# Softcap attention with a two-way maxout layer: w2's last two parts loaded in f32 and cast on VectorE, w1's loads spread, the w2 w_out product in another order

## Chip, cores and metric

One core of one Trainium2 chip. The metric is the time of one execution on the device, in microseconds (us): the median over runs of the same kernel. The engines are named as the profile names them: PE (TensorE, matrix products), PEld (its weight loads), DVE (VectorE), ACT (ScalarE), POOL (GpSimd), SP (SyncE, which here only issues transfers).

## The reference

For each of 8 batches and 12 heads (448 rows, head size 64): `scores = 30 * tanh(q k^T / 8 / 30)`, a softmax over the keys, times `v`. The heads are put side by side into `x` of 3584 x 768. Then, with `w1` and `w2` of 768 x 1024 and `w_out` of 1024 x 768:

```python
h1 = x @ w1
h2 = x @ w2
g = np.maximum(h1, h2)
return (g @ w_out).astype(np.float32)
```

Inputs and output are float32.

## The kernel before

**The second layer is rewritten.** max(h1, h2) = h2 + relu(h1 - h2), so the output is x (w2 w_out) + relu(x (w1 - w2)) w_out. The kernel makes the two weight matrices once, at the start: `wd_sb` = w1 - w2 in bf16 (`subtract`, L224, on POOL, one instruction for each of KC = 6 parts of 128 rows) and `wm_sb` = w2 w_out (`premultiply`, L237, on PE: 16 matmuls for a part, in two halves of 8, each evicted by DVE at L248). A part of w2 must be turned before it can be the weight operand: `turn_w2` (L229) is 8 transposes on PE into one PSUM tile "mm" and a DVE copy into `w2T` (L235). "mm" and `w2T` have two buffers each, so a new half can only start when the eviction two tiles back is done.

**Where the weights lie.** w2 in bf16 (`w2b`) borrows the one buffer of `gT`, which the second layer's relu (L410) writes later. w1 in f32 has no tiles of its own: parts 0 to 3 (OB = 4) lie in the four "osb" buffers, parts 4 and 5 in the first "xT" buffer (`w1x`). w2 comes by POOL's software queue, which casts on the way (L216); w_out too (L207); w1 by SP (L222).

**Attention.** The 48 pairs of heads are taken in 24 steps t of two pairs, and q, k, v are loaded, cast to bf16 and turned in groups g of three pairs (0 and 1 in wide rows, the others as rows of 768 and 256 bytes, L130 to L143). Groups 0 and 1 are turned on PE (L273). From group 2 on, POOL casts k and q (L183 to L195) and SP starts a DMA transpose, the crossbar (`cross`, L279), which fills `qkT`; the step's score matmuls (L306, L301) wait for it. Step 3 is the first that needs group 2, and the second tile of step 4 the first that needs group 3. ACT takes tanh (L307, L309) and exp (L314) of each tile; `total` (L343) and `values` (L364) make the row sums and the products with v on PE, DVE normalizes (L394) into `xT`.

**What sets the order.** The schedule is written out by hand: every engine runs its instructions in program order, and waits only by data and buffers. Filler work for PE sits in a list `fill_q` of generators, and `F(n)` takes n matmuls from its head. In the first steps the list holds turn and premultiply of parts 1 to 5, turn always one part ahead; from step 2 on the second layer is appended (L406 is x times `wd_sb`, whose first tile reads all six parts one after another; L418 and L421 make the output; L425 evicts it).

**SP's queue around the change:** k, q, v of groups 0 and 1; k and q of group 2; all six parts of w1 (L519); the transpose of group 2 (L565); k, q of group 3; v of group 2; the transpose of group 3 (L595); v of group 3; the groups 4 and 5. Each of SP's transfers also waits for the one eight places before it, since they share eight semaphores in turn.

**POOL's queue around the change:** issue of w2 parts 0 and 1 and of w_out (L490 to L493); casts of group 1; issue of w2 parts 2 to 5 (L513); v of groups 0 and 1; k, q of group 2; subtract parts 0 to 3 (L624); k, q of group 3; subtract parts 4 and 5 (L596); v of groups 2 and 3; then, after a one-element copy that waits for a step's `xT` (`mark`, L641), the next groups.

Of the kernel before, what the change touches and what calls it, by code (L numbers as in the profile page):

```python
# [10 lines left out]
def kernel(  # L11
# [11 lines left out]
    nc = tc.nc  # L23
    f32 = mybir.dt.float32
# [7 lines left out]
    DF = moe_w1.shape[1]  # L32
    P = 128
# [85 lines left out]
    def load(g, what, n0=0, n1=L):  # L119
        b, p = divmod(g * L, NP)  # L120
        h0, h1 = 2 * (p + n0), 2 * (p + n1)
        src = {"k": k, "q": q, "v": v}[what]
        t, m, l = raw_of(g, what)
        if g < NT:
            nc.sync.dma_start(
                out=t[:, n0 * S : n1 * S].rearrange("p (n c) -> p n c", c=S),
                in_=rows(src, b, h0, h1).rearrange("(n p) c -> p n c", p=P),
            )
            return
        nc.sync.dma_start(  # L130
            out=m[:, 2 * n0 : 2 * n1, :],
            in_=src[b, h0:h1, 0 : NJ * P, :].rearrange("h (p j) d -> p h (j d)", j=NJ),
        )
        if what == "q":
            nc.sync.dma_start(
                out=l[half(b), 2 * n0 : 2 * n1, :],
                in_=src[b, h0:h1, NJ * P : S, :].rearrange("h p d -> p h d"),
            )
        else:
            for par in range(2):  # L140
                nc.sync.dma_start(
                    out=l[64 * par : 64 * par + 64, n0:n1, :],
                    in_=src[b, h0 + par : h1 : 2, NJ * P : S, :].rearrange("h p d -> p h d"),  # L143
                )
# [72 lines left out]

    w1x = xpool.tile([P, NP, 2 * S], bf16, name="xT").rearrange("p c s -> p (c s)").bitcast(f32)

    def load_w1(c):  # L220
        w1_in[c] = opool.tile([P, DF], f32, name="osb") if c < OB else w1x[:, (c - OB) * DF : (c - OB + 1) * DF]
        nc.sync.dma_start(out=w1_in[c], in_=x_rows(moe_w1, c))  # L222

    def subtract(c, eng=nc.vector):  # L224
# [4 lines left out]
    def turn_w2(c):  # L229
        ps = mm_psum.tile([P, 512], f32, name="mm").bitcast(bf16)  # L230
        for f in range(FC):
            nc.tensor.transpose(ps[:, f * P : (f + 1) * P], w2b[:, c, f * P : (f + 1) * P], ident)
            yield
        w2T[c] = stage.tile([P, FC * P], bf16, name="w2T", bufs=2)
        nc.vector.tensor_copy(w2T[c], ps)  # L235

    def premultiply(c):  # L237

        for half in range(2):
            hs = slice(half * (DM // 2), (half + 1) * (DM // 2))  # L240
            ps = mm_psum.tile([P, 512], f32, name="mm")
            for f in range(FC):
                nc.tensor.matmul(  # L243
                    ps[:, : DM // 2], w2T[c][:, f * P : (f + 1) * P], wo_sb[:, f, hs],
                    start=(f == 0), stop=(f == FC - 1),
                )
                yield
            nc.vector.tensor_copy(wm_sb[:, c, hs], ps[:, : DM // 2])  # L248
# [149 lines left out]
    def moe(b):  # L398
        if b % 2 == 0:
            gT[b // 2] = xpool.tile([P, FC, 2 * S], bf16, name="gT", bufs=1)  # L400
        g, x = gT[b // 2], xT[b // 2]
        cs = slice((b % 2) * S, (b % 2 + 1) * S)
        for f in range(FC):
            ps = mm_psum.tile([P, 512], f32, name="mm")
            for c in range(KC):
                nc.tensor.matmul(  # L406
                    ps[:, :S], wd_sb[:, c, f * P : (f + 1) * P], x[:, c, cs], start=(c == 0), stop=(c == KC - 1)
                )
                yield
            nc.vector.tensor_relu(g[:, f, cs], ps[:, :S])  # L410
        for t in range(3) if b % 2 == 0 else range(3, 7):
            osb = opool.tile([P, DF], f32, name="osb")[:, :DM]
            ts = slice(t * P, (t + 1) * P)
            for half in range(2):
                hs = slice(half * (DM // 2), (half + 1) * (DM // 2))
                ps = mm_psum.tile([P, 512], f32, name="mm")
                for c in range(KC):
                    nc.tensor.matmul(ps[:, : DM // 2], x[:, c, ts], wm_sb[:, c, hs], start=(c == 0), stop=False)  # L418
                    yield
                for f in range(FC):  # L420
                    nc.tensor.matmul(  # L421
                        ps[:, : DM // 2], g[:, f, ts], wo_sb[:, f, hs], start=False, stop=(f == FC - 1)
                    )
                    yield
                nc.vector.tensor_copy(osb[:, hs], ps[:, : DM // 2])  # L425
                if b == B - 1 and t == 6:
                    o = out[b * S : b * S + NJ * P, hs].rearrange("(p j) n -> p j n", j=NJ)
                    nc.sync.dma_start(out=o[:, NJ - 1, :], in_=osb[:, hs])
            if b == B - 1 and t == 6:
                continue  # L430
            wide = b * NP >= NT * L
            if t == 3:
                for n in range(2):
                    o = out[(b - 1 + n) * S : (b + n) * S, :]
                    to = o[NJ * P : S, :] if (b - 1 + n) * NP >= NT * L else o.rearrange("(r j) n -> r j n", j=R7)[:, R7 - 1, :]
                    nc.sync.dma_start(out=to, in_=osb[64 * n : 64 * n + 64, :])
            else:
                j = t if t < 3 else t - 4
                o = out[b * S : (b + 1) * S, :]
                if wide:  # L440
                    nc.sync.dma_start(out=o[: NJ * P, :].rearrange("(p j) n -> p j n", j=NJ)[:, j, :], in_=osb)
                else:
                    o = o.rearrange("(r j) n -> r j n", j=R7)
                    for n in range(2):
                        nc.sync.dma_start(out=o[:, 2 * j + n, :], in_=osb[64 * n : 64 * n + 64, :])
# [4 lines left out]
    def F(n):  # L450
        rate[1] += n * rate[0]
        while rate[1] >= 1 and fill_q:
            try:
                next(fill_q[0])
                rate[1] -= 1
            except StopIteration:
                fill_q.pop(0)
        if not fill_q:
            rate[1] = 0.0
# [50 lines left out]
    ex(0, 3)  # L510
    cast(nc.gpsimd, 1, "k")
    cast(nc.gpsimd, 1, "q")
    for c in range(2, KC):  # L513
        load_w2(c)
    cast(nc.gpsimd, 0, "v", halves=(1,))
    load(1, "v")
    load(2, "k")
    load(2, "q")
    for c in range(KC):  # L519
        load_w1(c)  # L520

    first = {}

# [41 lines left out]
    cross(2)  # L565
    load(3, "k")
    load(3, "q")
    load(2, "v")
    premultiply_first(6, 8)
    for c in range(1, KC):  # L570
        if c + 1 < KC:
            fill_q.append(turn_w2(c + 1))
        fill_q.append(premultiply(c))
    scores(2, 0)
    ex(1, 3)
    total(0)
# [4 lines left out]
    for t in range(1, NQ):  # L581
        i = 2 * t
        more = t + 1 < NQ
        F(24 if t == 2 else 0)
        if t > 1 and more:
            scores(t + 1, 0)
        if t > 1:
            ex(t, 3)
            F(6)
        if t in crosses:  # L590
            cross(crosses[t])
        if t == 2:
            cast(nc.gpsimd, 3, "k")
            cast(nc.gpsimd, 3, "q")
            cross(3)  # L595
            for c in range(4, KC):  # L596
                subtract(c, nc.gpsimd)
        if t == 3:
            cast(nc.gpsimd, 3, "v")
        if t > 2:  # L600
            extra(i)
        F(8 if t > 1 else 0)
        add(t, 1, 0)
        F(2 if t > 1 else 0)
        if more:
            scores(t + 1, 1)
            ex(t + 1, 0)
        F(4)
        add(t, 1, 1)
        F(4)  # L610
        if t == 2:
            cast(nc.gpsimd, 2, "v")
            load(3, "v")
        add(t, 0, 2)
        F(4)
        add(t, 1, 2)
        F(4)
        if more:
            scores(t + 1, 2)
            ex(t + 1, 1)  # L620
            F(5)
            add(t + 1, 0, 0)
        if t == 1:
            for c in range(4):  # L624
                subtract(c, nc.gpsimd)
        if t == 2:
            extra(4)
            extra(5)
        if t > 2:
            extra(i + 1)  # L630
        F(5)
        total(t)
        if more:
            scores(t + 1, 3)
            ex(t + 1, 2)
            add(t + 1, 0, 1)
        else:
            F(12)
        normalize(t, values(t))
        if casts[t]:  # L640
            nc.gpsimd.tensor_copy(mark, x_of(t, 1)[:1, :1])  # L641
            for g, what in casts[t]:
                cast(nc.gpsimd, g, what)
        if t % 3 == 2:
            fill_q.append(moe(t // 3))
        F(3)
    F(10 ** 9)
# [33 lines left out]
```

## Time and profile before

| | us |
|---|---|
| median of 8 runs | 359.2 (357.57 to 359.94) |
| the profiled execution | 357.57 |
| its span in the profile | 355.8 |
| PE busy | 332.7 (93%) |
| ACT busy | 281.7 (79%) |
| DVE busy | 227.2 (64%) |
| POOL busy | 109.4 (31%) |

The span runs from the first to the last instruction of the profiled execution; some 1.8 us of its time lie around it. Busy shares are means over unlike stages: in most steps PE and ACT take turns as the engine that the other waits for, and after ACT's last exp the rest of the second layer keeps PE busy alone. The granted PE clock is full in nearly all of the 40 slices, with two slower places, in the early steps and around the seventh slice. The 16 DMA engines are busy most of the time in the first half, and move 61.79 MB in all: 58.21 MB on SP's queue and 3.15 MB on POOL's.

### The profile page before, as it was taken

The numbers are of one execution on the slowest core, as the hardware profiler recorded it, in microseconds if no ns is written. First come the engines' busy times: TensorE is split into PE (matmuls) and PEld (weight loads), VectorE is DVE, ScalarE is ACT, GpSimd is POOL, SyncE is SP. The second block draws the span as 40 slices with busy tenths as digits, with TensorE's granted clock in tenths as the row PEclk, the third lists the DMA queues.
The fourth block names the chain that finished last, engine by engine and source line by source line (L and its number), as shares of the span: only waits on it lengthen the run. The fifth ranks groups of instructions, "written<-read, shape, count | busy, mean of one in ns | idle before, by whom it ended". The sixth has DMA issues, their size and how long they took to land.

```text
span 355.8 us, 6788 instructions
## 1 busy us (share of the span) xinstructions
PE 332.7 (93%) x2710; PEld 162.2 (46%) x2710; DVE 227.2 (64%) x410; ACT 281.7 (79%) x265; POOL 109.4 (31%) x172
## 2 busy tenths in 40 slices
PE   3779869999999999999999999999999999999996
PEld 2434424444444444444444554354445444455563
DVE  5335617886877685777678665976696668833421
ACT  3999549999999999999999999899999999200000
POOL 6743858333134214312440343034304400000000
PEclk9989989999999999999999999999999999999999
DMA  7999999967994879666967598949873521012022
GB/s 253 259 250 244 339 243 156 273 143 185 172 288 108 211 157 302 166 154 130 291 189 168 93 272 248 211 89 270 250 169 66 147 86 51 0 46 89 0 90 88
DMA packets 103200, 61.79 MB, mean 174 GB/s; under 512 B 62336, under 2 KB 98176, under 8 KB 103168
## 3 DMA queue, kind: packets, MB, share of 16 engines
q1 hardware_dynamic: 101216, 58.21, 63.8%
q0 software_dynamic: 1952, 3.15, 4.8%
q8 instruction: 21, 0.34, 0.4%
q14 instruction: 11, 0.09, 0.1%
HBM read 42.47 MB, written 11.01 MB: 150 GB/s over the span
## 4 chain that ended last, share of the span: by engine, by line
PE 45%; ACT 33%; DMA 12%; DVE 8%; issue 1%; POOL 0%; SPq 0%; ACTq 0%; POOLq 0%
ACT expo L314 16%; ACT tanh L307 15%; PE mm L406 14%; PE mm L421 10%; PE mm L418 8%; DMA kr<-in_k_dram 7%; PE s L306 4%; DMA qkT<-kqf 3%; ACT tanh L309 3%; PE pv L372 2%; DVE gT L410 2%; PE mm L243 2%; PE ss L372 2%; DMA osb<-in_moe_w_dram 2%; DVE esum L333 1%
## 5 line engine op out<-in xcount | busy, mean ns | idle before, releaser
L314 ACT ACTIVATE expo<-tanh 128x1792 bf16<-128x1792 bf16 (+1 forms) x96 | 144.8, 1509 | 0.1
L307 ACT ACTIVATE tanh<-s 128x896 bf16<-128x896 f32 x144 | 124.2, 914 | 18.3 <-PE s L306 16.4
L421 PE MATMUL mm<-wo_sb,gT 128*128 128x384 bf16 x448 | 86.8, 327 | 0.0
L406 PE MATMUL mm<-xT,wd_sb 128*128 128x448 bf16 x384 | 80.2, 353 | 3.1 <-DVE gT L410 1.6
L418 PE MATMUL mm<-wm_sb,xT 128*128 128x384 bf16 x336 | 66.7, 327 | 0.2 <-DVE gT L410 0.2
L421 PEld LDWEIGHTS <-gT 128*128 128x128 bf16 x448 | 42.0, 98 | 34.2 <-issue 8.0
L406 PEld LDWEIGHTS <-wd_sb 128*128 128x128 bf16 x384 | 35.9, 98 | 43.2 <-issue 12.4
L425 DVE COPY osb<-mm 128x384 f32<-128x384 f32 x56 | 31.0, 554 | 37.0 <-PE mm L421 36.6
L306 PE MATMUL s<-qkT 64*128 64x448 bf16 x288 | 42.9, 366 | 9.3 <-DMA qkT<-kqf 4.9
L410 DVE TENSOR_SCALAR gT<-mm 128x448 bf16<-128x448 f32 x64 | 39.7, 621 | 14.1 <-PE mm L406 13.7
L335 DVE TENSOR_TENSOR esum<-expo 128x896 bf16<-128x896 bf16 x42 | 27.5, 654 | 32.6 <-ACT expo L314 32.1
L641 POOL COPY mark<-xT 1x1 bf16<-1x1 bf16 x18 | 3.3, 181 | 144.2 <-DVE xT L394 121.8
L418 PEld LDWEIGHTS <-xT 128*128 128x128 bf16 x336 | 31.8, 98 | 26.7 <-issue 6.6
L337 DVE TENSOR_TENSOR esum<-esum,expo 128x896 bf16<-128x896 bf16 x42 | 27.0, 643 | 0.3
L333 DVE TENSOR_TENSOR esum<-esum,expo 64x896 bf16<-64x896 bf16 x42 | 26.3, 627 | 0.9
L309 ACT ACTIVATE tanh<-s 128x896 bf16<-128x896 f32 x24 | 22.0, 916 | 3.8 <-PE s L301 3.2
L306 PEld LDWEIGHTS <-qkT 64*128 64x128 bf16 x288 | 9.5, 95 | 32.7 <-issue 25.2
L358 DVE STREAM_TRANSPOSE st<-ss 128x448 f32<-128x448 f32 x24 | 15.6, 650 | 8.9 <-PE ss L356 6.2
L372 PEld LDWEIGHTS <-vp 128*32 128x32 bf16 x576 | 13.2, 96 | 16.5 <-issue 8.5
L183 POOL CAST kqf<-kr 128x1152 bf16<-128x1152 f32 x14 | 15.9, 1139 | 9.3 <-DMA kr<-in_k_dram 9.1
L372 PE MATMUL pv<-expo,vp 128*32 128x448 bf16 x288 | 18.1, 356 | 0.0
L372 PE MATMUL ss<-expo,vp 128*32 128x448 bf16 x288 | 17.8, 352 | 0.0
(70 smaller groups left out, 272.2 us busy)
## 6 DMA issues: line engine op xcount, KB each, us to landing
kr<-in_k_dram SPq DMA_DIRECT2D x14, 576.0 KB, 7.1
qr<-in_q_dram SPq DMA_DIRECT2D x14, 576.0 KB, 7.2
vr<-in_v_dram SPq DMA_DIRECT2D x14, 576.0 KB, 5.0
out_dram<-osb SPq DMA_DIRECT2D x20, 384.0 KB, 4.6
out_dram<-osb SPq DMA_DIRECT2D x16, 192.0 KB, 4.2
osb<-in_moe_w_dram SPq DMA_DIRECT2D x4, 512.0 KB, 9.3
gT<-in_moe_w_dram POOLq DMA_DIRECT2D x6, 256.0 KB, 13.1
wo_sb<-in_moe_w_out_dram POOLq DMA_DIRECT2D x4, 384.0 KB, 16.0
```

The lines of the kernel that those rows point to most:

```text
L306: nc.tensor.matmul(s[:, h, :S], k0[r, j * P : (j + 1) * P], qTn[r, :])
L307: nc.scalar.activation(tanh[t, p][:, 2 * m : 2 * m + 2, :], s[:, :, :S], AF.Tanh, scale=scale / cap)
L309: nc.scalar.activation(tanh[t, p][:, 0:2, :], s[:, :, :S], AF.Tanh, scale=scale / cap)
L314: nc.scalar.activation(expo[t, p], tanh[t, p][:, 0:n, :], AF.Exp, scale=float(cap))
L333: nc.vector.tensor_add(d, d, expo[t, 2][r, :, :])
L335: nc.vector.tensor_add(d, e_of(t, ab, 1 if ab else 0), e_of(t, ab, 2 if ab else 1))
L372: nc.tensor.matmul(ps[r, :S], vp[g % 2][:, 2 * n + h, j, u::2], e_of(t, ab, j)[:, h, :], start=(j == 0), stop=False,)
L406: nc.tensor.matmul(ps[:, :S], wd_sb[:, c, f * P : (f + 1) * P], x[:, c, cs], start=(c == 0), stop=(c == KC - 1))
L410: nc.vector.tensor_relu(g[:, f, cs], ps[:, :S])
L418: nc.tensor.matmul(ps[:, : DM // 2], x[:, c, ts], wm_sb[:, c, hs], start=(c == 0), stop=False)
L421: nc.tensor.matmul(ps[:, : DM // 2], g[:, f, ts], wo_sb[:, f, hs], start=False, stop=(f == FC - 1))
L425: nc.vector.tensor_copy(osb[:, hs], ps[:, : DM // 2])
```

## The change

w2's parts 4 and 5 no longer come through POOL's casting queue. SP loads them as f32 into the two places in the first "xT" buffer that w1's parts 4 and 5 had, and DVE casts them into `w2b` at the end of step 1. Only then does SP load w1's parts 4 and 5 into the same places. Ahead of the transpose of group 2, SP now issues four weight parts (w2's 4 and 5, w1's 0 and 1) where it issued six; w1's parts 2 and 3 follow behind k and q of group 3, then w1's 4 and 5, then v of group 2. POOL subtracts parts 0 and 1 in step 1 and parts 2 to 5 in step 2, behind k, q and the transpose of group 3. In PE's filler list turn 4 comes behind premultiply 3, and turn 5 behind premultiply 4.

```diff
@@ beside load_w1 @@
+    def w1x_of(c):
+        return w1x[:, (c - OB) * DF : (c - OB + 1) * DF]
+
+    def load_w2_wide(c):
+        nc.sync.dma_start(out=w1x_of(c), in_=x_rows(moe_w2, c))
+
     def load_w1(c):
-        w1_in[c] = opool.tile([P, DF], f32, name="osb") if c < OB else w1x[:, (c - OB) * DF : (c - OB + 1) * DF]
+        w1_in[c] = opool.tile([P, DF], f32, name="osb") if c < OB else w1x_of(c)
         nc.sync.dma_start(out=w1_in[c], in_=x_rows(moe_w1, c))
@@ the first steps @@
-    for c in range(2, KC):
+    for c in range(2, OB):
         load_w2(c)
     cast(nc.gpsimd, 0, "v", halves=(1,))
     load(1, "v")
     load(2, "k")
     load(2, "q")
-    for c in range(KC):
-        load_w1(c)
+    for c in range(OB, KC):
+        load_w2_wide(c)
+    load_w1(0)
+    load_w1(1)
@@ before the loop over the steps @@
     cross(2)
     load(3, "k")
     load(3, "q")
-    load(2, "v")
+    load_w1(2)
+    load_w1(3)
     premultiply_first(6, 8)
-    for c in range(1, KC):
-        if c + 1 < KC:
-            fill_q.append(turn_w2(c + 1))
-        fill_q.append(premultiply(c))
+    for f, c in (
+        (turn_w2, 2), (premultiply, 1), (turn_w2, 3), (premultiply, 2), (premultiply, 3),
+        (turn_w2, 4), (premultiply, 4), (turn_w2, 5), (premultiply, 5),
+    ):
+        fill_q.append(f(c))
@@ step 2, behind cross(3) @@
-            for c in range(4, KC):
+            for c in range(2, KC):
                 subtract(c, nc.gpsimd)
@@ step 1 @@
-            for c in range(4):
+            for c in range(2):
                 subtract(c, nc.gpsimd)
@@ end of a step @@
+        if t == 1:
+            for c in range(OB, KC):
+                nc.vector.tensor_copy(w2b[:, c, :], w1x_of(c))
+                load_w1(c)
+            load(2, "v")
         F(3)
```

## Prediction

> **What bounds the kernel now.** I read the chain of waits first, in order of time, since the change touches the first 60 us only.
>
> ```profile
> 7.66 25.30 DMA kr<-in_k_dram
> 32.97 5.63 DMA osb<-in_moe_w_dram
> 38.60 9.36 DMA qkT<-kqf
> 48.00 0.93 PE s L306 x4
> 48.93 3.44 PE mm L243 x14
> ```
>
> Columns: start, length, what. Until 48.00 the end hangs on DMA: k and q of group 2, then 9.36 us of group 2's transpose. The second transpose needs 7.4 us from issue to landing (smallest in the `kqf` view). The timeline then shows who pays (last bracket: idle time before, and its cause).
>
> ```profile
> 36.86 1.15 POOL L183 CAST kqf<-qr 128x1152 bf16<-128x1152 f32 x1 [1.91 <-DMA qr<-in_q_dram]
> 38.07 0.51 POOL L188 CAST kqf<-qr 64x384 bf16<-64x384 f32 x1
> 38.60 7.29 SPq L279 DMA_TRANSPOSE qkT<-kqf  x1
> 38.78 8.37 POOL L225 TENSOR_TENSOR wd_sb<-osb,gT 128x1024 bf16<-128x1024 f32 x4 [0.20 <-DMA osb<-in_moe_w_dram]
> 42.64 0.48 PE L243 MATMUL mm<-wo_sb,w2T 128*128 128x384 bf16 x2 [0.20 <-DVE wm_sb L248]
> 48.00 0.93 PE L306 MATMUL s<-qkT 64*128 64x448 bf16 x4 [4.88 <-DMA qkT<-kqf]
> 48.66 1.73 ACT L307 ACTIVATE tanh<-s 128x896 bf16<-128x896 f32 x2 [7.72 <-PE s L306]
> 48.86 3.51 PE L243 MATMUL mm<-wo_sb,w2T 128*128 128x384 bf16 x14
> 54.54 1.15 POOL L183 CAST kqf<-qr 128x1152 bf16<-128x1152 f32 x1 [1.56 <-DMA qr<-in_q_dram]
> 56.34 4.61 POOL L225 TENSOR_TENSOR wd_sb<-xT,gT 128x1024 bf16<-128x1024 f32 x2
> 59.49 1.93 DVE L337 TENSOR_TENSOR esum<-esum,expo 128x896 bf16<-128x896 bf16 x1
> ```
>
> PE stands 4.88 us and ACT 7.72 us. Behind the stall PE is slow as well: 14 matmuls in 3.51 us, where 16 took 2.92 us at 39.08, and four L306 in 0.93 us instead of 0.55. That is 0.95 + 0.38 = 1.3 us; the stretches by window say why.
>
> ```profile
> 36.00:40.00 4.00, 4.00 (x61) 1.89 (x60) 3.11 (x7) 3.97 (x5) 2.88 (x3) 1.00 1.02 371
> 40.00:44.00 4.00, 2.92 (x22) 1.56 (x19) 2.19 (x4) 0.94 (x2) 4.00 (x3) 1.00 1.37 343
> 44.00:48.00 4.00, 0.00 (x0) 0.00 (x1) 0.00 (x0) 0.00 (x0) 3.15 (x2) 0.95 0.93 195
> 48.00:52.00 4.00, 4.00 (x17) 1.76 (x18) 0.56 (x1) 3.31 (x3) 0.86 (x1) 0.62 0.91 265
> ```
>
> Columns: window, length, busy time (and count) of PE, PEld, DVE, ACT, POOL; granted clock, DMA share, GB/s. The clock falls to 0.62 behind the empty window. From 48 to 78 PE stands for 0.33 us only, and from 77.49 ACT sets the pace; later waits hang on the kernel's own steps, so what is won by 77.5 stays to the end.
>
> **What the change does to the transpose of group 2.** (1) Two parts leave POOL's queue. By the page that queue used 4.8% of 16 engines' span, 17.1 us, for 3.15 MB; a part of 0.26 MB is 1.4 us, two are 2.8 us. All this was ahead of or beside k and q of group 2, and the DMA share is 1.0 to 1.14 from 8 to 36 us, so I let q land 2.8 us earlier, at 34.1 instead of 36.86 (bounds: 0, if the parts only filled gaps, and 2.8). POOL's casts of q took 1.72 us, so the transpose is issued at 35.8 instead of 38.60. (2) In SP's queue four 0.52 MB parts stand before it, not six. At the 371 and 343 GB/s of 36 to 44 us a part costs 1.45 us; two are 2.9 us. Together 48.0 - 2.8 - 2.9 = 42.3; the issue plus the second transpose's 7.4 us gives 43.2, which I take.
>
> **When PE gets there.** Before, PE reached L306 of step 3 at 43.1 and waited. Now two things hold it longer. Eight matmuls (1.3 us by 2.92 us for 16) stand before it in place of eight transposes (0.61 us at 41.67): +0.7 us. And DVE has two new casts, 128x1024 f32 to bf16, right behind normalize (ends 39.88). Nearest rows: DVE's L174, 128x896, took 0.63 us, scaled 0.72; L156, 64x576, took 1.29 us for two, scaled 1.15. I take 0.72, the wider tile. Queued behind them is the w2T copy of part 3 (L235), which frees an "mm" buffer; PE's second half of premultiply 2 started at 40.53 right when it ended. With casts until 41.3 and 0.68 us for the copy it starts at 42.0, and 18 matmuls at 0.165 us end at 45.0.
>
> The casts can also meet POOL. The row at 59.49 is an esum add of 1.93 us, whose median is 0.61, while a subtract ran from 58.80 to 60.94: it stood until POOL was done. The first two subtracts (2.12 us each) now start when w1's part 0 lands, some 37 to 38, and so run over 39.88. I charge half a subtract, 1.1 us, with bounds of 0 and 2.1. PE then reaches step 3 at 46.1 (45.0, and 48.0 with slow casts and a full subtract), later than the transpose's 43.2: 1.9 us won.
>
> The Trainium skill (SBUF — State Buffer, "Who interferes with whom") speaks against this placement: casts with source and target in SBUF may use the port pair that VectorE shares with GpSimd, and whichever starts second stands for the whole of the other's instruction. The row above is an add with two inputs, so no row shows this for a cast; by the page the wait is the rest of a subtract, by the undisturbed L174 row it is nothing, and the sum would be 1.1 us worse or better than mine at most.
>
> **Behind step 3's scores.** PE has the 0.7 us less to do there that it did earlier. The slow clock cost 1.3 us behind a gap of 4.88 us, and none behind the gap of 1.46 us at 24.67. The new gap (40.5 to 43.1) lies between; I count half, 0.65 us won (0 to 1.3). ACT bounds the two together: its idle time from 48.66 to 77.5 was 2.1 us. Sum 1.35 us.
>
> **POOL's chain, where the cost lies.** Four subtracts, not two, now follow k and q of group 3, and the second layer's first L406 tile reads part 5 as its sixth matmul, at 63.00 + 5 x 0.21 = 64.05 before. The loads of k and q 3 stand right behind the transpose; q landed at 54.54, 6.6 us after it, so now at 43.2 + 6.6 = 49.8. Casts end at 51.5. The two subtracts at 56.34 took 4.61 us, so four take 9.2 us (8.5 at 2.12): part 5 is ready at 60.7, against a need at 64.05 - 3.25 = 60.8. Just covered. Group 3's transpose is issued at 51.5 instead of 56.28, but w1's parts 2 to 5 (5.8 us) and v of group 2 (0.69 MB, 2.6 us at 265 GB/s) are now ahead of it: from 49.8 they last to 58.2, and the transpose's own 3.8 us (issue time at 56.28) end at 62.0. Its user, the second tile of step 4 (64.42 + 0.28 before), would want it at 61.5. A stall of 0.5 us.
>
> **Costed at nothing.** Two software issues less on POOL (1.1 us): POOL then waited 1.49 us for v anyway. v of group 2, now cast behind part 5 to 63.0: first used by step 3's values at 71.20 - 3. SP's new waits (w1's part 4 for the casts and for the first transpose's landing, part 5 for k 3, v's last piece for q 3) all end before 50 and hold only one another, since the next transpose waits for POOL until 51.5. The relu that overwrites w2 waits for the last subtract: 65.24 - 3 against 60.7.
>
> **The sum.** 1.9 + 1.35 - 0.5 = 2.75 us. From the profiled execution's 357.57 that gives 354.8; this execution was the fastest of eight, and against the median, 359.2, it is 356.4, which I forecast.
>
> **Rivals.**
> - *Only the shorter queue counts.* Were q of group 2 not earlier, the transpose would land at 48.0 - 2.9 = 45.1, still before PE's 46.1, but q 3 at 51.7, part 5 at 51.7 + 1.7 + 9.2 = 62.6, 1.8 us after its need: 3.25 - 1.8 = 1.45 won, 357.7. For it: SP issues slowly (11.63 us for two small loads at 8.07). Against: the DMA share above 1. Chance 0.2.
> - *VectorE's casts take the place of the wait.* Step 3 at 48.0, slow clock again, only the 0.7 us: 358.5. For it: row 59.49, and a late w1 part 0. Chance 0.15.
> - *POOL's chain makes it slower.* If k and q 3 land no earlier than before (54.54), four subtracts end at 54.54 + 1.7 + 9.2 = 65.4 and PE, which runs in order, stands at L406 1.4 us past the old time: 360.6. It decides from q 3's landing: beyond 53.2 the change loses. For it: these loads are issued behind a transpose that held SP 7.29 us. Against: everything ahead of them shrinks. Chance 0.15.
> - *Better than forecast.* No meeting with POOL and a full clock: 3.0 + 2.0 without stall = 5.0, 354.2. Part of the forecast's case, which has 0.5 in all.
>
> **How the numbers follow.** The forecast with its open terms spans 354.2 to 357.5; the low end takes 0.9 us more, less than half of the eight runs' spread of 2.4 us: 353.3. The high end takes in POOL's chain: 360.7. About 0.3% (1.1 us) is what this kernel's measurement can tell. Faster by more: all of the forecast's 0.5 and most of the first rival's, 0.65. Within: the second rival and the rest, 0.19. Slower: POOL's chain and a little, 0.16.
>
> **What would show it.** Right: q cast near 34, transpose issued near 36 and landed by 44; PE's L306 of step 3 near 46 with its gap now before L243, released by DVE; clock mostly full from 48. Wrong: DVE's casts over 1.5 us each, or L406 waiting for `wd_sb`, or scores of step 4 waiting for `qkT`. If k and q 3 land after 53 the forecast is wrong in sign.

## The result, and the profile after

| | before | after |
|---|---|---|
| median | 359.15 us (356.29 to 360.90) | 363.08 us (359.84 to 364.00) |
| ratio, 95% interval | | 1.0102 [1.0080, 1.0124] |
| the profiled execution | 357.57 | 360.94 |
| its span | 355.8 | 359.1 |

The change costs 3.9 us where 2.8 us were forecast as won; 363.08 lies outside the forecast's range, whose upper end was 360.7. The profiles differ by 3.4 us, and the kernel after has other line numbers: L241 is the w2T copy (L235 before), L249 premultiply (L243), L231 the subtract (L225), L312 the scores (L306), L412 the second layer's first product (L406), L658 the new casts, whose target w2b has the name gT and whose source the name xT.

First the chain of waits of the kernel after (start, length, what). The transpose is gone from it; VectorE's casts and the slow matmuls behind them are new:

```profile
33.90 2.11 PE mm L249 x13
41.06 3.79 DVE gT L658 x2
45.50 5.73 PE mm L249 x18
51.63 1.73 ACT tanh L313 x2
```

Its timeline (start, length, engine and line; last bracket: idle time before, and its cause):

```profile
35.27 1.15 POOL L183 CAST kqf<-qr 128x1152 bf16<-128x1152 f32 x1 [1.30 <-DMA qr<-in_q_dram]
...
37.02 4.64 SPq L285 DMA_TRANSPOSE qkT<-kqf  x1
39.64 4.66 POOL L231 TENSOR_TENSOR wd_sb<-osb,gT 128x1024 bf16<-128x1024 f32 x2 [2.65 <-DMA osb<-in_moe_w_dram]
...
40.25 1.46 PE L249 MATMUL mm<-wo_sb,w2T 128*128 128x384 bf16 x8
40.97 3.87 DVE L658 CAST gT<-xT 128x1024 bf16<-128x1024 f32 x2
44.77 0.68 DVE L241 COPY w2T<-mm 128x1024 bf16<-128x1024 bf16 x1
45.50 5.73 PE L249 MATMUL mm<-wo_sb,w2T 128*128 128x384 bf16 x18 [3.79 <-DVE w2T L241]
51.16 0.55 PE L312 MATMUL s<-qkT 64*128 64x448 bf16 x4
51.63 1.73 ACT L313 ACTIVATE tanh<-s 128x896 bf16<-128x896 f32 x2 [9.24 <-PE s L312]
...
53.31 0.68 DVE L241 COPY w2T<-mm 128x1024 bf16<-128x1024 bf16 x1
54.05 0.50 PE L249 MATMUL mm<-wo_sb,w2T 128*128 128x384 bf16 x2 [0.80 <-DVE w2T L241]
...
58.85 0.68 DVE L241 COPY w2T<-mm 128x1024 bf16<-128x1024 bf16 x1
59.60 0.82 PE L249 MATMUL mm<-wo_sb,w2T 128*128 128x384 bf16 x4 [1.36 <-DVE w2T L241]
...
65.89 1.30 PE L412 MATMUL mm<-xT,wd_sb 128*128 128x448 bf16 x6
```

Read from the top: q of group 2 is cast and its transpose issued 1.6 us earlier than before (36.86 and 38.60), and PE's scores at 51.16 no longer wait for it. But the two casts stand on VectorE from 40.97 to 44.8, beside POOL's two subtracts (39.64 to 44.30). Behind them the w2T copy is late, PE stands 3.79 us, and then its 18 matmuls take 5.73 us where 16 took 2.92 us before. Step 3's scores start at 51.16 instead of 48.00, and ACT stands 9.24 us instead of 7.72. Further on PE stands twice more, 0.80 and 1.36 us, for a w2T copy. The second layer starts at 65.89 instead of 63.00.

The stretches by window (window, length, busy time and count of PE, PEld, DVE, ACT, POOL; granted clock, DMA share, GB/s) show the clock at half for longer than before:

```profile
40.00:44.00 4.00, 1.71 (x17) 0.85 (x10) 4.00 (x4) 2.39 (x3) 4.00 (x2) 1.00 1.10 152
44.00:48.00 4.00, 2.50 (x8) 1.13 (x8) 1.91 (x3) 0.00 (x0) 1.36 (x2) 0.51 0.98 284
48.00:52.00 4.00, 4.00 (x18) 1.66 (x17) 1.11 (x2) 0.37 (x1) 2.31 (x5) 0.64 1.08 342
```

From step 3's normalize on the kernels differ by less than 1 us. In all 17 profiles of this case 36.3 to 36.4 us lie between the normalize of step 3 and that of step 6, and 246.5 to 247.3 us from there to the end. So a profile's span is settled by when step 3's normalize starts: 72.9 before, 75.8 after.

### The profile page after: what moved, and what is told of

Same layout as the page of the kernel before. It is cut to its first block, busy times and chain, and to the rows that moved or that the text cites. A ratio compares the mean times of both kernels' runs of the same rounds, so it can differ in the third digit from the quotient of the medians.

```text
span 359.1 us, 6792 instructions
## 1 busy us (share of the span) xinstructions
PE 337.2 (94%) x2710; PEld 163.7 (46%) x2710; DVE 229.7 (64%) x412; ACT 281.7 (78%) x265; POOL 107.1 (30%) x170
## 4 chain that ended last, share of the span: by engine, by line
PE 48%; ACT 36%; DVE 8%; DMA 5%; issue 1%; POOL 1%; ACTq 0%; DVEq 0%
ACT expo L320 17%; ACT tanh L313 16%; PE mm L412 14%; PE mm L427 10%; PE mm L424 8%; DMA wo_sb<-in_moe_w_out_dram 4%; PE s L312 4%; PE mm L249 3%; ACT tanh L315 3%; PE pv L378 2%; PE ss L378 2%; DVE gT L416 2%; DVE esum L339 1%; PE s L307 1%; DVE gT L658 1%
## 5 line engine op out<-in xcount | busy, mean ns | idle before, releaser
L412 PE MATMUL mm<-xT,wd_sb 128*128 128x448 bf16 x384 | 80.2, 353 | 2.8 <-DVE gT L416 1.6
L412 PEld LDWEIGHTS <-wd_sb 128*128 128x128 bf16 x384 | 35.9, 98 | 42.8 <-issue 12.5
L312 PE MATMUL s<-qkT 64*128 64x448 bf16 x288 | 43.3, 368 | 3.9 <-ACT tanh L313 1.8
L343 DVE TENSOR_TENSOR esum<-esum,expo 128x896 bf16<-128x896 bf16 x42 | 25.6, 610 | 0.3
L249 PE MATMUL mm<-wo_sb,w2T 128*128 128x384 bf16 x80 | 17.3, 368 | 6.0 <-DVE w2T L241 6.0
L312 PEld LDWEIGHTS <-qkT 64*128 64x128 bf16 x288 | 9.7, 95 | 28.1 <-issue 25.9
L364 DVE STREAM_TRANSPOSE st<-ss 128x448 f32<-128x448 f32 x24 | 15.6, 650 | 10.3 <-PE ss L362 6.1
```

What stands on the lines that cost most here:

```text
L249: nc.tensor.matmul(ps[:, : DM // 2], w2T[c][:, f * P : (f + 1) * P], wo_sb[:, f, hs], start=(f == 0), stop=(f == FC - 1),)
L312: nc.tensor.matmul(s[:, h, :S], k0[r, j * P : (j + 1) * P], qTn[r, :])
L412: nc.tensor.matmul(ps[:, :S], wd_sb[:, c, f * P : (f + 1) * P], x[:, c, cs], start=(c == 0), stop=(c == KC - 1))
```

## The experiments

The theory from the profile after: two edits cost. (1) VectorE's casts meet POOL's subtracts and each waits for the other (**the lock**). (2) The new order of turn and premultiply puts 18 long matmuls, not 10 and 8 short transposes, between the gap and step 3's scores, and puts each late turn right ahead of its own premultiply, so that PE waits for the copy between them (**the order**). The rivals: POOL's chain of subtracts is the cost, or the split loads themselves. Each ratio is to runs of the kernel before on the same chip; where two kernels are compared below, the difference is that of their ratios, times 359 us, since the chips differ a little.

| kernel | median, us | ratio to before [95%] | step 1's normalize | step 3's normalize | span |
|---|---|---|---|---|---|
| before | 359.15 | 1 | 38.7 | 72.9 | 355.8 |
| after | 363.08 | 1.0102 [1.0080, 1.0124] | 39.9 | 75.8 | 359.1 |
| casts_later | 356.70 | 0.9934 [0.9911, 0.9956] | 40.1 | 73.3 | 356.6 |
| subs_later | 359.41 | 1.0020 [0.9997, 1.0043] | 39.6 | 75.2 | 358.5 |
| casts_act | 357.03 | 0.9948 [0.9929, 0.9968] | 38.6 | 71.8 | 355.3 |
| w2_by_pool | 357.20 | 0.9943 [0.9923, 0.9963] | 38.8 | 72.5 | 355.4 |
| order_only | 361.54 | 1.0076 [1.0051, 1.0100] | 39.2 | 75.9 | 358.8 |
| after_oldorder | 357.76 | 0.9978 [0.9962, 0.9994] | 39.3 | 72.5 | 355.7 |
| after_together | 359.01 | 0.9995 [0.9974, 1.0017] | 38.8 | 73.1 | 356.3 |
| after_turn4early | 359.33 | 1.0019 [1.0000, 1.0037] | 40.1 | 74.4 | 357.6 |
| act_oldorder | 358.00 | 0.9967 [0.9943, 0.9990] | 39.9 | 69.9 | 353.5 |
| before_together | 356.96 | 0.9951 [0.9933, 0.9969] | 40.4 | 73.0 | 355.8 |
| split_loads | 358.59 | 0.9994 [0.9972, 1.0015] | 39.6 | 75.0 | 357.9 |
| later_together | 355.56 | 0.9920 [0.9898, 0.9943] | 39.0 | 73.4 | 356.6 |
| act_together | 358.23 | 0.9982 [0.9958, 1.0007] | 40.0 | 70.0 | 353.5 |
| later_dve | 357.27 | 0.9950 [0.9929, 0.9971] | 39.6 | 70.8 | 354.0 |
| act_dve | 356.71 | 0.9960 [0.9941, 0.9979] | 38.9 | 71.3 | 354.8 |

The last three columns are of one profiled execution each; the runs of one kernel spread over 1.7 to 5.2 us, so such a row can stand at either end of them (act_oldorder's profile is its fastest run, 355.24, later_together's its slowest, 358.35).

### The lock: four ways to take it away

**casts_later** moves the casts, and what follows them, into step 2.

```diff
@@ step 2, behind F(24) @@
+        if t == 2:
+            for c in range(OB, KC):
+                nc.vector.tensor_copy(w2b[:, c, :], w1x_of(c))
+                load_w1(c)
+            load(2, "v")
@@ end of a step @@
-        if t == 1:
-            for c in range(OB, KC):
-                nc.vector.tensor_copy(w2b[:, c, :], w1x_of(c))
-                load_w1(c)
-            load(2, "v")
```

> The changed kernel with DVE's two casts of w2 (and the loads of w1's parts 4 and 5 and of v of group 2 that follow them) moved behind the 24 filler matmuls of step 2, so that they stand behind the w2T copy and the evictions that PE waits for, and at a time when POOL subtracts nothing. Theory (the casts stand behind POOL's subtracts on a shared lock, PE stands behind the casts, and the clock falls behind that gap): PE's 3.8 us gap at L249 goes, each cast takes some 0.55 us instead of 1.35 and 2.60, PE reaches the scores of step 3 near 45 instead of 51.2 with a full clock; about 5 us less than the changed kernel, 357.5 to 358.5 us. Rival (the late subtracts and the filler order are what costs): the gap goes, but what it wins is given back at L412 or behind the turns; 362 us or more.

**subs_later** leaves the casts where they are and moves POOL's first two subtracts behind them.

```diff
@@ step 2, behind cross(3) @@
-            for c in range(2, KC):
+            for c in range(KC):
                 subtract(c, nc.gpsimd)
@@ step 1 @@
-        if t == 1:
-            for c in range(2):
-                subtract(c, nc.gpsimd)
```

> The changed kernel with all six subtracts on POOL in step 2, so that none runs beside DVE's casts, which stay where they are. Theory of the lock: casts of some 0.55 us each, PE reaches the scores of step 3 near 45 to 46, but POOL ends part 5 some 4.3 us later, at 65, and PE then stands at L412 for 4 to 5 us: 361 to 362 us in all. Rival (casts are slow by themselves, 1.3 us or more, from their size): casts as slow as in the changed kernel, and 365 us or more with the later subtracts on top.

**casts_act** changes only the engine of the casts.

```diff
-                nc.vector.tensor_copy(w2b[:, c, :], w1x_of(c))
+                nc.scalar.copy(w2b[:, c, :], w1x_of(c))
```

> The changed kernel with one word changed: ACT, not DVE, casts w2's parts 4 and 5, at the same place in the program. Theory (the casts cost because DVE and POOL hold one lock, and what PE waits for stands behind them on DVE): PE has no gap at L249, reaches step 3 near 45 with a full clock, keeps the waits for the w2T copies of parts 4 and 5 (0.8 and 1.4 to 3 us); 357.5 to 360 us. Rival (the loads and the filler order alone make the changed kernel slow): within 1 us of the changed kernel, 362 to 364 us.

**w2_by_pool** keeps the rest of the change, and lets POOL's casting queue bring w2's parts 4 and 5 again; SP's f32 loads of these parts (`load_w2_wide`) go.

```diff
-    for c in range(2, OB):
+    for c in range(2, KC):
         load_w2(c)
...
-                nc.vector.tensor_copy(w2b[:, c, :], w1x_of(c))
```

> The changed kernel with w2's parts 4 and 5 cast by POOL's queue as before: no DVE casts, two w1 parts ahead of group 2's transpose, the new filler order. Theory: q of group 2 lands near 36.9 as in the kernel before, the transpose is issued near 38.6 and lands near 44, PE reaches step 3 near 45, w2T copies right behind their turns cost 2 us as in the changed kernel; 358 to 359.5 us. Rival (the late w1 parts and four subtracts behind group 3's casts cost by themselves): 361 us or more.

Measured: 356.70, 359.41, 357.03 and 357.20 us; by the ratios 0.8 to 1.7% less than after, 2.9 to 6.0 us. All four came out below what was expected, by 0.5 to 1.6 us. The ways have in common only that the casts and the subtracts no longer meet on VectorE and POOL. The cleanest is subs_later: the same casts, on the same engine, at the same place in the order, with POOL idle, in its timeline:

```profile
40.68 1.29 DVE L655 CAST gT<-xT 128x1024 bf16<-128x1024 f32 x2
...
42.62 3.08 PE L249 MATMUL mm<-wo_sb,w2T 128*128 128x384 bf16 x18 [1.20 <-DVE w2T L241]
```

Two casts take 1.29 us, not 3.87; PE's gap is 1.20 us, not 3.79, and the same 18 matmuls run at full clock, 3.08 us, not 5.73. In casts_act two casts on ACT beside the same subtracts took 1.99 us, 1.0 each (in act_together too). How the time is divided is read from the groups of L658 and L231 in the kernel after (shortest, median, longest in ns):

```profile
L658 DVE CAST gT<-xT x2: 1347/1976/2604, 41.0 to 42.2; 128x1024 bf16<-128x1024 f32 x2
...
L231 POOL TENSOR_TENSOR wd_sb<-osb,gT x4: 2127/2129/2557, 39.6 to 54.2; 128x1024 bf16<-128x1024 f32 x4
```

The first cast started at 40.97, 1.33 us into a subtract that ended at 41.77, and ended 0.55 us behind that; the second started at 42.2 and ended about 0.5 us behind the second subtract (44.30). That second subtract was itself 0.43 us longer than the first. The two take turns, each for a whole instruction. This is what the Trainium skill says (SBUF — State Buffer, "Who interferes with whom"), and here it holds for a cast too, as it did for an add. The page also exempts what has at most one input in SBUF and runs outside VectorE's two-port modes, which a cast can enter by the page. L254's casts from PSUM show no lock: they took 0.54 to 0.56 us beside subtracts and without.

subs_later paid a price, which was smaller than expected: six subtracts behind k and q of group 3 make L412 wait 0.83 and 1.72 us for `wd_sb`. Taking the lock from the casts does not end it. In casts_later it falls on the next VectorE instruction with two inputs in SBUF that meets a subtract, the esum add, and a w2T copy stands behind that one:

```profile
45.20 1.28 DVE L597 CAST gT<-xT 128x1024 bf16<-128x1024 f32 x2
...
52.10 2.34 DVE L341 TENSOR_TENSOR esum<-expo 128x896 bf16<-128x896 bf16 x1 [0.31 <-ACT expo L320]
...
55.09 0.82 PE L249 MATMUL mm<-wo_sb,w2T 128*128 128x384 bf16 x4 [3.08 <-DVE w2T L241]
```

The add takes 2.34 us in place of 0.63, and PE's wait for part 5's copy grows from 1.36 to 3.08 us.

### The order: added alone, and taken away alone

**order_only** puts the new order into the kernel before, **after_oldorder** the old order into the kernel after.

```diff
-    for c in range(1, KC):
-        if c + 1 < KC:
-            fill_q.append(turn_w2(c + 1))
-        fill_q.append(premultiply(c))
+    for f, c in (
+        (turn_w2, 2), (premultiply, 1), (turn_w2, 3), (premultiply, 2), (premultiply, 3),
+        (turn_w2, 4), (premultiply, 4), (turn_w2, 5), (premultiply, 5),
+    ):
+        fill_q.append(f(c))
```

> The kernel before with only the filler order changed (turn 4 behind premultiply 3, turn 5 behind premultiply 4). Theory: PE still waits for group 2's transpose to 48, which hides the 0.7 us more in front of it; behind it PE waits for the w2T copy of parts 4 and 5 (0.8 and 1.4 us in the changed kernel) and has 0.7 us less to do: 1 to 1.5 us slower than the kernel before. Rival (the order costs nothing, as the forecast took it): the same time within 0.5 us, or 0.7 us less.

> The changed kernel with the filler order of the kernel before (turn always one part ahead); loads, casts and subtracts as changed. Theory (order_only: the order costs 2.4 us, the casts the rest): PE still stands some 3.8 us behind the casts and runs slow behind it, but waits no more for w2T copies: 360 to 361.5 us. Rival (the order costs nothing here, since the gap covers it): 362.5 us or more.

Measured: 361.54, 0.76% or 2.7 us more than before (expected 1 to 1.5), and 357.76, 1.24% or 4.5 us less than after (5.3 by the medians; expected 1.6 to 3). Both times the order weighs more than I had allowed. In after_oldorder the lock and the gap are still there:

```profile
44.64 2.08 PE L249 MATMUL mm<-wo_sb,w2T 128*128 128x384 bf16 x8 [3.54 <-DVE w2T L241]
46.51 1.06 PE L238 MATMUL mm<-ident,gT 128*128 128x128 bf16 x8
47.37 0.84 PE L249 MATMUL mm<-wo_sb,w2T 128*128 128x384 bf16 x2
...
48.15 0.83 PE L312 MATMUL s<-qkT 64*128 64x448 bf16 x4
```

Behind a gap of 3.54 us, 3.5 us of slow work stand ahead of the scores, not 5.7, and no premultiply waits for its copy. In order_only, whose gap is the old wait for the transpose, the clock stood at half from 46.36 to 56.60 us, with the copy's wait in the midst of it:

```profile
48.00:52.00 4.00, 3.66 (x18) 1.69 (x14) 0.86 (x2) 3.31 (x3) 0.97 (x1) 0.50 1.00 282
52.00:56.00 4.00, 3.55 (x13) 1.19 (x14) 0.39 (x1) 2.14 (x3) 2.17 (x5) 0.50 0.88 216
```

### Which half of the order costs: the copies, or the slow matmuls?

**after_together** keeps the 18 matmuls and takes the copy waits away; **after_turn4early** is the old order up to the scores, and keeps part 5's copy wait.

```diff
@@ after_together @@
-        (turn_w2, 4), (premultiply, 4), (turn_w2, 5), (premultiply, 5),
+        (turn_w2, 4), (turn_w2, 5), (premultiply, 4), (premultiply, 5),
@@ after_turn4early @@
-        (turn_w2, 2), (premultiply, 1), (turn_w2, 3), (premultiply, 2), (premultiply, 3),
-        (turn_w2, 4), (premultiply, 4), (turn_w2, 5), (premultiply, 5),
+        (turn_w2, 2), (premultiply, 1), (turn_w2, 3), (premultiply, 2), (turn_w2, 4),
+        (premultiply, 3), (premultiply, 4), (turn_w2, 5), (premultiply, 5),
```

> The changed kernel with turn 5 right behind turn 4, ahead of premultiply 4, so that no turn is directly followed by its own premultiply; the 18 matmuls between the gap and step 3's scores stay. If the two copy waits (0.80 + 1.36 us) are what the order costs: some 2 us less than the changed kernel and more with the clock behind them, 359 to 361. If it is the 18 matmuls at half clock ahead of the scores: scores again at about 51, 362 to 363.

> The changed kernel with turn 4 back ahead of premultiply 3 (the old order until behind step 3's scores), turn 5 still behind premultiply 4. If the 18 matmuls at half clock are the cost: scores at about 48 and 358 to 359. If the copy waits are: that of part 5 stays, 1.4 of 2.2 us, so 360.5 to 362.

Measured: 359.01 and 359.33 us, by the ratios 3.8 and 3.0 us less than after. Each wins most of the 4.5 us alone, so neither "only the copies" nor "only the matmuls" holds, and the two are not a sum. The profile of after_turn4early shows how they are tied together:

```profile
38.49 4.23 POOL L231 TENSOR_TENSOR wd_sb<-osb,gT 128x1024 bf16<-128x1024 f32 x2 [2.39 <-DMA osb<-in_moe_w_dram]
...
41.18 2.69 DVE L658 CAST gT<-xT 128x1024 bf16<-128x1024 f32 x2
...
44.52 1.46 PE L249 MATMUL mm<-wo_sb,w2T 128*128 128x384 bf16 x8 [2.60 <-DVE w2T L241]
...
47.05 0.55 PE L312 MATMUL s<-qkT 64*128 64x448 bf16 x4
...
54.20 1.73 DVE L341 TENSOR_TENSOR esum<-expo 128x896 bf16<-128x896 bf16 x1 [0.43 <-ACT expo L320]
...
56.59 1.04 PE L249 MATMUL mm<-wo_sb,w2T 128*128 128x384 bf16 x4 [2.59 <-DVE w2T L241]
57.56 1.31 PE L355 MATMUL ss<-expo,ones 128*32 128x448 bf16 x12
```

The first gap, 2.60 us, is followed by full clock (8 matmuls in 1.46 us) and scores at 47.05, 4.1 us earlier than in after. Not all of that is the order's: nothing ahead of the gap was changed, but here the subtracts began at 38.49, the first was done before the casts began at 41.18, and only one cast met a subtract. The two took 2.69 us, not 3.87, so the gap was 1.2 us shorter before the order came into play. But part 5's copy now stands behind an esum add that meets a subtract, PE waits 2.59 us, and this gap of the same length is followed by half clock (12 of L355 in 1.31 us; 0.75 at full). In after_together the gap is as long as in after and the 18 matmuls still ran slowly:

```profile
44.36 4.42 PE L249 MATMUL mm<-wo_sb,w2T 128*128 128x384 bf16 x18 [3.80 <-DVE w2T L241]
```

But L412 starts at 61.94, 3.95 us earlier: 1.15 us from before the casts (step 1's normalize), 1.31 us less slow clock, and 2.16 us of copy waits gone, less 0.7 us of smaller waits. Only the last two stand where the edit is, some 1.5 us; the same 18 matmuls stood behind a gap of the same length in both kernels, so the edit does not explain the sooner clock (the last section does). How the order's 4.5 us divide between the copies and the slow matmuls is therefore not shown.

**act_oldorder** asks whether the order costs anything where the casts make no gap: casts on ACT, old order.

> Casts on ScalarE and the old filler order, all else of the change kept. No long gap ahead of step 3, so if the order costs only behind a gap: as the same kernel with the new order, 356.5 to 357.5. If the order costs by its copy waits (0.80 + 1.64 there): 354.5 to 355.5.

Measured 358.00 us, against 357.03 of casts_act with the new order, 0.5 us above the better of the two expected ranges, and the intervals overlap: no cost of the order is seen where the casts make no gap, though casts_act waits 0.80 and 1.64 us for copies. In act_oldorder these waits are gone, and PE stands 1.02 us at L412 for POOL's last subtract, and 0.75 us for group 3's transpose.

### What is left when PE is early: POOL's chain

**split_loads**: the kernel before with the loads and subtracts split, and nothing else (w2 by POOL, old order). **later_together**: casts_later with the order of after_together. **act_together**: casts_act with that order. **before_together**: that order in the kernel before.

> The kernel before with one part of the change alone: w1's parts 0 and 1 ahead of group 2's transpose, parts 2 and 3 behind k and q of group 3, parts 4 and 5 and v of group 2 behind them, four subtracts in step 2; w2 all through POOL's queue, the old filler order. Theory: the transpose lands near 45 instead of 48 and the gap stays under what lowers the clock; order_only put the new order at 2.4 us, so 357.2 - 2.4, 354.5 to 355.5 us. Rival (the order costs only where it meets the other parts): 357 us or more.

> casts_later with turn 5 right behind turn 4, ahead of premultiply 4. In casts_later PE stood 0.8 us for the w2T copy of part 4 and 3.1 us for that of part 5, which is behind step 3's first esum add on DVE; that add took 2.34 us beside a POOL subtract. Theory (the new filler order costs because a copy stands right between its turn and its premultiply, and the last one behind the add): both waits shrink to some 0.4 us in all, about 3 us off, 353.5 to 355 us. Rival (the wait for part 5 was cover for something else that is late, such as part 5 of wd_sb or group 3's transpose): 356 us or more, with a new wait at L412 or at the scores of step 4.

> The changed kernel with the two casts of w2 on ACT in place of DVE, where they stand in program order at the same place, and turn 5 right behind turn 4. ACT waits there for scores in all versions so far. Theory (the lock between DVE and POOL is what made the casts cost): ACT casts both in 2 to 2.2 us beside POOL's subtracts, PE has no gap at L249 and reaches step 3 near 45; 353.5 to 355.5 us. Rival (subtracts slow any reader of these tiles, or ACT loads another table): casts over 1.5 us each, or step 3's tanh late by 2 us or more; 357 us or more.

> The kernel before with turns 4 and 5 both between premultiply 3 and premultiply 4. Theory (in order_only the copies stood right between turn and use, and slow clock made it dearer): against order_only's +2.4 us this order costs at most 0.7 us more than the kernel before, 359 to 360 us. Rival (it is the eight premultiply matmuls moved ahead of step 3's scores that cost): 361 us or more as in order_only.

Measured: 358.59, 355.56, 358.23 and 356.96 us. split_loads was missed by 3 to 4 us, and its profile says why. PE has step 3's scores at 45.18, 2.8 us ahead of before, and gives it all back where the second layer first reads the late parts of `wd_sb`; behind these waits the clock is at half again (0.50 from 64 to 68 us):

```profile
59.17 4.58 POOL L231 TENSOR_TENSOR wd_sb<-xT,gT 128x1024 bf16<-128x1024 f32 x2
...
61.34 0.36 PE L412 MATMUL mm<-xT,wd_sb 128*128 128x448 bf16 x1 [1.63 <-POOL wd_sb L231]
...
63.80 0.93 PE L412 MATMUL mm<-xT,wd_sb 128*128 128x448 bf16 x2 [2.10 <-POOL wd_sb L231]
```

So the early transpose is worth little while four subtracts follow q of group 3. later_together pays the same at L412 (1.62 and 2.10 us) in its profiled run, which is its slowest, and still has the lowest ratio here, 0.8% or 2.9 us below before, with an interval that overlaps that of casts_later. act_together has one run of 355.27 and a median of 358.23, outside what was expected; its profile, taken on that run, cannot tell why the others are slower. before_together was expected to cost nothing or a little and wins 1.8 us. Ahead of the gap eight premultiply matmuls stand in place of eight transposes, as in order_only, and behind it no copy is waited for. The gap is 3.16 us in place of 4.88, but in that execution step 1's normalize was 1.7 us later too, and its span is that of before (355.8), so the profile does not show where the 1.8 us come from.

**later_dve** and **act_dve** take four of the subtracts from POOL to VectorE (parts 2 and 3 behind an esum add, 4 and 5 behind step 2's normalize), in later_together and act_together.

```diff
-            for c in range(2, KC):
-                subtract(c, nc.gpsimd)
...
+            if t == 2:
+                subtract(2)
+                subtract(3)
...
+        if t == 2:
+            subtract(4)
+            subtract(5)
```

> later_together with the four late subtracts on DVE: parts 2 and 3 behind step 3's first esum add, parts 4 and 5 behind step 2's normalize. In later_together PE stood 3.7 us at L412 for POOL's subtracts of 2.3 us each, and DVE's esum add took 2.36 us beside one. Theory (POOL's chain and its lock with DVE are the last of what the change cost): DVE takes 1.1 to 1.3 us for each, the wait at L412 shrinks under 1 us; 352 to 354.5 us. Rival (DVE has no room there; evictions and normalize come late instead): 355.5 us or more.

> act_together with the same four subtracts on DVE. act_together stood 1.0 us at L412 and 0.8 us for group 3's transpose in its profile, and its runs spread from 355.3 to 359.9 us. Theory as for later_dve: 354 to 356.5 us. Rival (what makes it slower than later_together is ACT's casts or the clock): 357.5 us or more.

Measured 357.27 (expected 352 to 354.5) and 356.71 us (expected 354 to 356.5): the first some 1.1 us worse than with POOL, the second 0.8 us better, both with overlapping intervals, so neither is settled. A subtract took about 1.2 us on VectorE, and PE now waited for VectorE: 1.82 and 1.08 us at L412, for the `wm_sb` evictions that stood behind the subtracts, and 1.77 and 2.25 us ahead of that, for step 2's row sums (L364), which stood behind the first two.

## Why the prediction was wrong

On the profiled execution's own base 354.8 us was forecast and 360.94 measured, 6.1 us apart. By the second layer's start (forecast 63.00 - 3.25 = 59.75, measured 65.89) the same 6.1 us are there, and they fall into four. (Behind that point the forecast lost 0.5 us, to group 3's transpose; the kernel lost 0.4 us, without a wait of that kind.)

- **Ahead of the change's place: 1.2 us.** Step 1's normalize started at 39.9, not 38.7. w_out's matmuls took 0.53 us each until 26.3 us in this execution, where before had 0.32 from 21.34 on. Over the 17 profiles this normalize starts between 38.6 and 40.4, in no order by edit (before_together, which changes nothing there, has 40.4). I count it as chance, and the forecast had no term for it.
- **The lock: 1.2 us more than charged.** "I charge half a subtract, 1.1 us, with bounds of 0 and 2.1": the casts and their waits took 3.79 us, against 1.44 + 1.1 = 2.54 in the sum. The mechanism was named; the size was not. One meeting was counted where two casts met two subtracts, so the bound of 2.1 was set for one meeting too. The text had the subtracts start at some 37 to 38, which leaves hardly more than the second for the casts; they started at 39.64, 1.33 us before the casts. In after_turn4early, where they started 2.7 us before, one meeting is what came. The cost over undisturbed casts was 3.87 - 1.29 = 2.6 us.
- **The clock behind the new gap: 2.7 us.** "The new gap ... lies between; I count half, 0.65 us won". The gap was expected at 40.5 to 43.1; it came at 41.7 to 45.5, and the clock was at half from 44.08 to 50.90. 18 matmuls took 5.66 us to the scores where 18 x 0.165 = 3.0 were counted. The order had made exactly this stretch longer, and the sum priced it at full clock alone ("in place of eight transposes (0.61 us at 41.67): +0.7 us").
- **The copy waits: 2.2 us, 1.1 net.** The text named turn 4 and turn 5 and their new places, and never asked what lies between a turn and its premultiply: a 0.68 us copy on VectorE (0.80 us of PE's time), and for part 5 a copy behind an esum add that waits for ACT's exp (1.36 us). Against the 2.16 us stand about 1 us that were saved beyond the forecast's count: no slow clock behind the scores any more (0.65 counted, 1.3 saved), and the 0.33 us wait of before.

The rest of the steps. The **shorter queues** were right in direction: q cast at 35.27 (34.1 forecast), the transpose issued at 37.02 (35.8) and landed before PE came; where PE did wait for it, in casts_act and later_together, scores started at 44.04 and 44.27, against 43.2 forecast and 48.00 before, with 7.7 us from issue to landing where 7.4 were taken. **POOL's chain** was right: q of group 3 cast at 50.35 (49.8), last subtract done at 60.9 (60.7), and no wait for `wd_sb` in after, though only because PE came 6 us late; in split_loads and later_together the same chain costs 3.7 us, so its cover was as thin as the forecast called it. Group 3's transpose made no wait in after, 2.01 us in casts_act.

Of the rivals, "VectorE's casts take the place of the wait" was the right one, at 0.15 and 358.5 us. It had scores at 48.0 as its worst case; they came at 51.16, 3.2 us later. Its slow casts and full subtract cover the casts as measured; what it lacks is the late start (1.2 us) and the 18 matmuls at half clock, which it too had at full clock. In the timed runs the two edits overlap: without the lock after wins 2.9 to 6.0 us, without the order 4.5 us, and these are not a sum, which fits each making the other dearer: the lock makes the gap, and the order puts more work behind it. The split loads by themselves are worth at most 1.0 us (split_loads, lower end of its interval).

What stays open: the length of a gap does not say whether or for how long the clock falls (last section), so the 2.7 us can't be called the price of a 3.8 us gap in every run; how the order's cost divides; and why the medians of act_together and act_oldorder lie 3 us above their profiled runs.

## What to carry to other kernels

Before an instruction with its operands in SBUF is put on VectorE, count every subtract that POOL runs in the same stretch: each meeting cost up to the rest of a subtract here (some 2 us), and what stands behind on VectorE (an eviction, a copy) carries it to PE. When filler work is put in another order, price it at the clock that will hold there, and look between each pair of producer and consumer for the copy on the other engine. A transfer that lands 3 us earlier is worth only what the next chain leaves of it, here POOL's subtracts.

## What the runs showed of the hardware that was not expected

- **Gaps of the same length, different clock.** In after_turn4early two gaps of 2.60 and 2.59 us were followed by full and by half clock. A gap of 3.08 us in casts_later was followed by 0.57 in the next window of 4 us, one of 3.13 us in subs_later by 1.00. The Trainium skill (TensorE: Matmul & The Clock Gate, "Part 1: The HAM clock gate (the "warmup" mystery)") tells of an activity window of 3.4 us that runs freely, and that the same work can fall differently into it.
- **The traces show that window.** Read in slices of 0.15 us, the granted clock of the 17 profiles has 24 slow stretches in the first 75 us, and each lasts 3.41, 6.83 or 10.25 us, that is one, two or three times 3.41. Where an execution has two, their starts lie a whole number of times 3.41 us apart (30.72 in before, 34.13 in after_turn4early). So each execution has its own grid of 3.41 us on which the clock changes. The first gap of after_turn4early is split by it: PE was busy for 1.93 us from 39.99 to 43.40 and for 2.08 from there to 46.81. The second lies in one window, with 0.82 us of busy PE from 53.64 to 57.05, and half clock followed. Behind each grid's first change, up to 300 us, all windows at full clock with at most 1.51 us of busy PE were followed by half clock, and all with 1.52 or more by full clock. The page's table lets the clock fall after an idle window; these windows were not idle, so here the measurement decides.
- **Slow time comes in whole windows.** After's gap ended at 45.50, late in its window, with PE busy for 1.99 us of 44.08 to 47.49, and a second slow window followed; after_together's ended at 44.36, with 2.74 us of 43.69 to 47.10, and the clock was full again. In order_only the 0.79 us wait for a copy lay in the second of three slow windows, with 2.63 us. No sharp line came out here: a slow window with 2.94 us in after_oldorder was followed by another.
- **The granted clock's column can be silent.** In the kernel after it shows 1.00 from 16 to 28 us, where w_out's matmuls took 0.53 us instead of 0.32. The duration of a known matmul is the surer sign.
